# Layer two's two products by one level of Strassen's algorithm

## The chip, the cores and the metric

The kernel runs on one core of a Trainium2 chip. The metric is the device time of one execution in microseconds (us), as the median of several runs. The core's engines are TensorE (PE: matmuls, into PSUM), VectorE (DVE), ScalarE (ACT) and GpSimd (POOL); SyncE (SP) issues all DMAs here. Each engine works off its own queue in order, and waits on semaphores for the others.

## The reference

Attention over chunks of 32 tokens, with 4 x 8 heads of 768 tokens, gives 3072 rows of 512 numbers. Two feed-forward layers follow, each with 512 x 2048 and 2048 x 512 weights, all in float32:

```python
x = attn_out.transpose(0, 2, 1, 3).reshape(B * S, H * D)      # 3072 x 512
h = x @ w_in1;  g = np.maximum(0.01 * h, h);  x = g @ w_out1  # layer one
h = x @ w_in2                                                 # layer two
g = h * np.clip(h + 3.0, 0.0, 6.0) / 6.0
return (g @ w_out2).astype(np.float32)
```

## The kernel before

**Numbers.** Every operand of a feed-forward matmul is split in two parts, a high one in a rounded format that PE takes at full pace and the low remainder; a product is three matmuls (high x high, high x low, low x high), made by `mm3` (L607 to L609). A matmul has 128 x 128 weights and 512 moving columns.

**Tiling.** The 3072 tokens are 6 blocks of 512 (`blk`), the 2048 hidden features are 16 slices of 128 (`f`). A step (`layer, blk, f`) is a hidden product `hidden` (4 slices of the inner dimension x 3 = 12 matmuls into one PSUM bank `ph`), an activation on ACT and DVE (`act_1` to `act_4`, L625 to L655) that leaves the two parts `gh` and `gl`, and the output product `output` (12 matmuls into four banks `py`, which gather over the 16 steps of a block). PE runs hidden(n), then output(n - 1). `done` and `stored` copy the four banks out and store them, in layer one to `y_dram`, from where `load_y`, `split_yh` and `split_yl` fetch a block for layer two.

**Weights.** `convert` loads each 128 x 512 piece of the weights, 64 in all, which come as the bits of float64 numbers, turns them to float32 with two ACT and four DVE instructions, and splits them (`w_high`, `w_low`). The 16 slices of a layer stay in SBUF (ring `w`); layer two's are converted during the last block of layer one and the first steps after it.

**Attention.** While PE works on block b of layer one, ACT, DVE and GpSimd prepare block b + 1; PE is lent to them in short visits (`visit`).

**Order.** `Program` (L45) is a list scheduler in the kernel's own text: every step has an engine, a planned length (table `TIME`), a due time, steps that it comes after, and places in rings of buffers that it takes and frees. `order` plays this plan through and emits the instructions of each engine in the planned order; on the chip only the order is kept, and the waits are the real ones.

## Time and profile before

| | us |
|---|---|
| median of 3 runs (1135.38 to 1135.52) | 1135.45 |
| span of the profiled execution | 1133.9 |
| PE busy | 1121.4 |
| DVE busy | 589.1 |
| ACT busy | 463.7 |
| GpSimd busy | 60.4 |
| DMA moved | 78.65 MB |

The profiled execution lies 1.55 us under the median, since its span runs from the first to the last instruction only. Busy time of PE is no measure of its pace: matmuls overlap, and each is shown with its own end. The distance between equal events of a repeating pattern is.

### The profile page before, as it was taken

The numbers are of one execution on the slowest core, as the hardware profiler recorded it, in microseconds if no ns is written. First come the engines' busy times: TensorE is split into PE (matmuls) and PEld (weight loads), VectorE is DVE, ScalarE is ACT, GpSimd is POOL, SyncE is SP. The second block draws the span as 40 slices with busy tenths as digits, with TensorE's granted clock in tenths as the row PEclk, the third lists the DMA queues.
The fourth block names the chain that finished last, engine by engine and source line by source line (L and its number), as shares of the span: only waits on it lengthen the run. The fifth ranks groups of instructions, "written<-read, shape, count | busy, mean of one in ns | idle before, by whom it ended". The sixth has DMA issues, their size and how long they took to land.

```text
span 1133.9 us, 16167 instructions
## 1 busy us (share of the span) xinstructions
PE 1121.4 (99%) x6375; PEld 921.9 (81%) x6375; DVE 589.1 (52%) x1280; ACT 463.7 (41%) x1043; POOL 60.4 (5%) x123
## 2 busy tenths in 40 slices
PE   8999999999999999999999999999999999999998
PEld 6777788888888888888888888888888888888887
DVE  6999865465665556656998623223223223222222
ACT  7888732334333343335777423223223223222222
POOL 4111110001000001000000000000000000000000
PEclk9999999999999999999999999999999999999999
DMA  8656421121111122115455102002002001001001
GB/s 261 193 173 188 148 75 38 38 88 63 38 56 57 48 65 76 38 64 185 150 150 179 62 1 75 1 1 75 1 1 75 1 1 38 1 1 38 1 1 38
DMA packets 31661, 78.65 MB, mean 69 GB/s; under 512 B 3424, under 2 KB 3424, under 8 KB 31584
## 3 DMA queue, kind: packets, MB, share of 16 engines
...
## 4 chain that ended last, share of the span: by engine, by line
PE 91%; DVE 4%; ACT 2%; DMA 1%; issue 1%; POOL 1%; SPq 0%; POOLq 0%; DVEq 0%
PE py L609 44%; PE ph L609 44%; PE px L472 2%; PE psc L346 1%; ACT e L422 1%; DMA raw<-in_moe_w_in_dram 1%; DVE w L259 1%; DVE wa L240 1%; DVE raw L247 1%; DVE wa L229 0%; DVE wa L233 0%; POOL e L441 0%; DVE gl L651 0%; DMA raw<-in_moe_w_out_dram 0%; ACT w L253 0%
## 5 line engine op out<-in xcount | busy, mean ns | idle before, releaser
L609 PE MATMUL ph<-xh,w 128*128 128x512 f32 x768 | 254.6, 392 | 0.0
L609 PE MATMUL ph<-yh,w 128*128 128x512 f32 x768 | 252.0, 389 | 0.0
L609 PE MATMUL py<-gh,w 128*128 128x512 f32 x768 | 239.2, 392 | 1.0 <-DVE w L259 1.0
L609 PE MATMUL py<-w,gh 128*128 128x512 f32 x768 | 236.4, 389 | 0.0
L637 DVE SCALAR_TENSOR_TENSOR ph<-g,ph 128x512 f32<-128x512 f32 x96 | 66.8, 696 | 294.1 <-ACT g L631 294.1
L631 ACT ACTIVATE g<-ph,three 128x512 f32<-128x512 f32 x96 | 66.2, 690 | 300.0 <-PE ph L609 299.7
L609 PEld LDWEIGHTS ph<-xh,w 128*128 128x128 f32 x768 | 143.9, 188 | 30.9 <-DVE w L259 0.4
L609 PEld LDWEIGHTS py<-gh,w 128*128 128x128 f32 x768 | 142.9, 188 | 31.6 <-DVE w L259 1.7
L609 PEld LDWEIGHTS ph<-yh,w 128*128 128x128 f32 x768 | 144.2, 188 | 29.9
L609 PEld LDWEIGHTS py<-w,gh 128*128 128x128 f32 x768 | 144.2, 188 | 29.9
L609 PE MATMUL ph<-xl,w 128*128 128x512 f32 x384 | 149.6, 390 | 0.8 <-DVE xl L494 0.8
L609 PE MATMUL py<-gl,w 128*128 128x512 f32 x384 | 149.6, 390 | 0.0
L609 PE MATMUL py<-w,gl 128*128 128x512 f32 x384 | 149.4, 389 | 0.0
L609 PE MATMUL ph<-yl,w 128*128 128x512 f32 x384 | 149.4, 389 | 0.0
L628 ACT ACTIVATE ph<-ph 128x512 f32<-128x512 f32 x96 | 55.9, 582 | 179.7 <-PE ph L609 179.5
L451 DVE STREAM_TRANSPOSE aT<-e 32x128 f32<-32x128 f32 x384 | 115.9, 302 | 16.4 <-POOL e L441 11.0
L651 DVE TENSOR_TENSOR gl<-ph,gh 128x512 fp32r<-128x512 f32 x96 | 66.3, 690 | 73.2 <-ACT gh L642 72.2
L653 DVE SCALAR_TENSOR_TENSOR gl<-ph,gh 128x512 fp32r<-128x512 f32 x96 | 66.4, 691 | 55.6 <-ACT gh L644 55.6
L609 PEld LDWEIGHTS ph<-xl,w 128*128 128x128 f32 x384 | 72.1, 188 | 15.6 <-DVE xl L494 1.1
L609 PEld LDWEIGHTS py<-gl,w 128*128 128x128 f32 x384 | 72.1, 188 | 15.1
L609 PEld LDWEIGHTS py<-w,gl 128*128 128x128 f32 x384 | 72.0, 187 | 15.1
L609 PEld LDWEIGHTS ph<-yl,w 128*128 128x128 f32 x384 | 72.0, 188 | 15.0
...
## 6 DMA issues: line engine op xcount, KB each, us to landing
...
y_dram<-yo SPq DMA_DIRECT2D x24, 256.0 KB, 2.0
...
out_dram<-oo SPq DMA_DIRECT2D x24, 256.0 KB, 2.8
...
```

The costliest lines, as they stand in the source:

```text
L240: nc.vector.scalar_tensor_tensor(out=a, in0=hi, scalar=0xC0000000, in1=a, op0=ALU.bitwise_and, op1=ALU.bitwise_or)
L247: nc.vector.tensor_tensor(out=hi, in0=tmp_t.pop(key), in1=lo, op=ALU.add)
L259: nc.vector.tensor_tensor(out=w[:, io, 1, :], in0=a, in1=w[:, io, 0, :].bitcast(F32), op=ALU.subtract)
L346: nc.tensor.matmul(pt[j][n * PT:(n + 1) * PT, m * W:(m + 1) * W], qt[r, hp, :], kt[r, hp, :], start=not more, stop=True, tile_position=(e ...
L451: nc.vector.transpose(out=t[c, :, r], in_=e[r, :, c])
L472: nc.tensor.matmul(pt[e * D:(e + 1) * D, at + hp * every:at + hp * every + PT], vt[:, c], t[:, hp, n * PT:(n + 1) * PT], start=True, stop= ...
L609: nc.tensor.matmul(dst, a, b, start=first and i == 0, stop=last and i == len(terms) - 1)
L628: nc.scalar.activation(out=ph, in_=ph, func=AF.Prelu, alpha=0.01)
L631: nc.scalar.activation(out=g, in_=ph, func=AF.Relu, bias=three, scale=1.0)
L637: nc.vector.scalar_tensor_tensor(out=ph, in0=g, scalar=6.0, in1=ph, op0=ALU.min, op1=ALU.mult)
L651: nc.vector.tensor_sub(out=gl, in0=ph, in1=gh.bitcast(F32))
L653: nc.vector.scalar_tensor_tensor(out=gl, in0=ph, scalar=1.0 / 6.0, in1=gh.bitcast(F32), op0=ALU.mult, op1=ALU.subtract)
```

## The change

Layer one is computed as before. Layer two goes through its 6 blocks as 3 stages of two blocks (1024 tokens). Each of its two products is cut into 2 x 2 blocks, and 7 products of sums of these blocks take the place of 8 (in Winograd's form, with four sums of each operand).

**Weight sums.** `combine` (16 times, during blocks 1 to 4 of layer one) loads two pieces of layer two's weights, converts them, makes four sums of 128 x 256, and stores the seven operands in `w_dram`. `add_weights` fetches them two at a time as `cw0` to `cw27` when layer one's slots in `w` come free, splits them on ACT and DVE for the hidden product, and later on ACT and GpSimd for the output.

**Activation sums.** `add_x` loads 1024 tokens of `y_dram` into four tiles `rows0` to `rows3`, and makes the seven operands in place with four `mix` on DVE, each split by `high` (ACT) and `low` (DVE) of 128 x 1024 into `fb8`, `x0` to `x3`, `xwa`, `xwb`.

**Hidden products.** `add_hidden`: for a group of two pairs of feature slices (banks k = 0 and 1), products 0 to 6 go to banks B, A, E, B, E, B, D. Copies of B and E on ACT (`copied`) and sums on DVE (`summed`) give the four blocks of h; `gate` (ACT) and `gate_by` (DVE) make the activation, GpSimd a difference of two of them, and four results go to `g_dram`. Five buffers `gated` pass them on.

**Output products.** `add_outputs`: all hidden products of the three stages come first, then the outputs. The operands come from `g_dram`, with 12 `mix` a stage, and are split by ACT and DVE into three rotating tiles (`SPIN`). Weights are the stationary operand here too, so the result stands transposed: `turned_out` transposes 32 x 32 blocks on DVE, and `out_store` stores four DMAs with pieces of 64 numbers. The host lays out `w_out2` to suit.

```diff
-    rings = dict(w=NF, raw=NRAW, wa=2, ye=4, aT=2, gh=2, gl=2, x=2, py=4, ph=2, pa0=1, pa1=1, qk=1, v=1, yn=1)
+    rings = dict(w=2 * NF, raw=NRAW, wa=2, ye=4, aT=2, g=2, x=4, py=4, ph=2, pa0=1, pa1=1, qk=1, v=1)
...
+    PROD, LETTERS, FINAL = 7, "BAEBEBD", "ABEAEAD"
...
+    def h_product(p, i, c):
+        dst = sums(LETTERS[i], p % 2)
+        n = p * PROD + i
+        w, (xh, xl) = combined(n // 2)[:, n % 2], wide(c)
+        for k in range(2):
+            wh, wl = (w[:, h, k * P:(k + 1) * P] for h in range(2))
+            mm(dst, wh, xh[:, k, :], i in (0, 1, 2, 6) and k == 0)
+            mm(dst, wh, xl[:, k, :], False)
+            mm(dst, wl, xh[:, k, :], False)
+    def o_product(i, q, c):
+        w, (xh, xl) = combined(i * NQ // 2 + q // 2)[:, q % 2], wide(c)
+        for m in range(2):
+            dst = sums(FINAL[i], m)
+            wh, wl = (w[:, h, m * P:(m + 1) * P] for h in range(2))
+            mm(dst, wh, xh[:, q % 2, :], i in (0, 1, 2, 6) and q == 0)
+            mm(dst, wh, xl[:, q % 2, :], False)
+            mm(dst, wl, xh[:, q % 2, :], False)
+    def copied(n, letter, k):
+        nc.scalar.copy(out=small(n), in_=sums(letter, k))
+    def summed(letter, k, n, out):
+        b, t = sums(letter, k), small(n)
+        nc.vector.tensor_tensor(out=t if out else b, in0=b, in1=t, op=ALU.add)
...
+    def gate(letter, k, n):
+        nc.scalar.activation(out=gated(n), in_=sums(letter, k), func=AF.Relu, bias=half, scale=1.0 / 6.0)
+    def gate_by(letter, k, n):
+        g = gated(n)
+        nc.vector.scalar_tensor_tensor(out=g, in0=g, scalar=1.0, in1=sums(letter, k), op0=ALU.min, op1=ALU.mult)
+    def g_differ(a, b):
+        nc.gpsimd.tensor_tensor(out=gated(a), in0=gated(b), in1=gated(a), op=ALU.subtract)
...
+    def turned_out(k, n, m):
+        t = fixed(f"gated{k}", [P, 2, 512], "g", 2).rearrange("p a c -> p (a c)").rearrange("p (j m b) -> p j m b", j=16, m=2)
+        nc.vector.transpose(out=t[:, :, m, :], in_=small(n).rearrange("p (j b) -> p j b", b=32))
+    def out_store(k, s, n, h, i):
+        t = fixed(f"gated{k}", [P, 2, 512], "g", 2).rearrange("p a c -> p (a c)").rearrange("p (j e) -> p j e", j=16)
+        at = (2 * s + n) * TB
+        dst = out[at:at + TB, P * i + 64 * h:P * i + 64 * (h + 1)].rearrange("(j a) e -> a j e", a=32)
+        nc.sync.dma_start(out=dst, in_=t[32 * i:32 * (i + 1)])
...
+    def combine(p, io, t):
+        hold = [max((x for x in paced if x[0] <= t - 10))[1]]
+        mixed, b = [], None
+        was = [("wa", (1, 2 * p + e, io)) for e in range(2)]
+        for e in range(2):
+            key = (1, 2 * p + e, io)
+            r = ("raw", 2 + e)
+            u = t + 4 * e + LATER
+            first = [("raw", ("f", e))] if p == io == 0 else []
+            cell("SP", T["load"], u - LATER - 9, w_load, *key, after=hold, takes=first, writes=[r], nbytes=P * 4096)
+            b = cell("ACT", T["words"], u - 4.9, w_upper, key, after=[b], reads=[r], takes=was[e:e + 1])
+            l = cell("ACT", T["words"], u - 4.2, w_lower, key, writes=[r])
+            c = add("DVE", T["clip"], u - 4.2, w_clip, key, after=[b])
+            c = add("DVE", T["shift"], u - 3.7, w_shift, key, after=[c])
+            c = cell("DVE", T["join"], u - 3.2, w_join, key, after=[c], reads=[r])
+            mixed.append(cell("DVE", T["add"], u - 2.4, w_add, key, after=[c, l], reads=[r]))
+        m = ("raw", 2)
+        c = cell("DVE", T["quarter"], t + LATER + 2.5, c_first, p, io, after=mixed, writes=[m])
+        for n in range(3):
+            c = cell("DVE", T["quarter"], t + LATER + 3.0 + 0.5 * n, c_more, p, io, n, writes=[m], frees=was if n == 2 else ())
+        c_stored[io, p] = []
+        for n in range(4):
+            c_stored[io, p].append(
+                cell("SP", T["load"], t + 3.0 + 0.5 * n, c_store, p, io, n, after=mixed, reads=[m] if n > 1 else [],
+                     frees=was[n:n + 1], nbytes=P * (1024 if n == 1 - io else 2048))
+            )
...
+    WIDE = ["fb8", "x0", "x1", "xwa", "xwb", "x2", "x3"]
+    SPIN = ["xwa", "xwb", "fb8"]
+    def add_weights(io, t, need):
+        w = [("cw", t)]
+        pairs = {(2 * t + e) // PROD if io == 0 else (2 * t + e) % NQ for e in range(2)}
+        cell("SP", T["load"], need - 24, cw_load, io, t, writes=w, nbytes=P * 2048,
+             **merged(own("w", f"cw{t}"), dict(after=[x for p in pairs for x in c_stored[io, p]])))
+        cell("ACT", T["high"], need - 9, cw_high, t, writes=w)
+        if io == 0:
+            cell("DVE", T["low"], need - 8, cw_low, t, nc.vector, writes=w)
+        else:
+            cell("POOL", T["pool"], need - 8, cw_low, t, nc.gpsimd, writes=w)
+    def add_wide(src, c, need):
+        cell("ACT", T["wide_copy"], need - 4.0, high, src, c, reads=[src], writes=[c], **wide_own(c))
+        cell("DVE", T["wide"], need - 2.9, low, src, c, reads=[src], writes=[c])
...
+    def add_x(s):
+        t = hidden_at[s] - (14 if s == 0 else 3)
+        R = [("raw", j) for j in range(4)]
+        for j in (0, 2, 1, 3):
+            k, n = j // 2, j % 2
+            cell("SP", T["load"], t - 24 + j, rows_load, s, j, writes=[R[j]], nbytes=P * 4096,
+                 after=[attended] + [evicted[2 * s + n, 2 * k + e] for e in range(2)])
...
+        split(0, 0)
+        split(1, 2)
+        mixed(2, 1, 3, 1, ALU.subtract)
+        split(2, 1)
...
+    def add_hidden(s, pairs, t0):
+        keep = {}
+        for i in range(PROD):
+            for p in pairs:
+                k = p % 2
+                t = t0 + (2 * i + k) * H6
+                b, e = [(LETTERS[i], k)], t + H6
+                last = s == NS - 1 and p == NF // 2 - 1 and WIDE[i].startswith("x") and not WIDE[i].startswith("xw")
+                cell("PE", H6, t, h_product, p, i, WIDE[i], reads=[("cw", (p * PROD + i) // 2), WIDE[i]], writes=b,
+                     frees=[("x", WIDE[i])] if last else (), **bank_own(LETTERS[i], k))
+                n = {0: SA, 2: SA, 3: SB, 5: SC}.get(i)
+                if n:
+                    cell("ACT", T["copy"], e, copied, n[k], LETTERS[i], k, reads=b, writes=[n[k]], **small_own(n[k]))
+                n = {1: SA, 4: SB, 5: SA, 6: SC}.get(i)
+                if n:
+                    cell("DVE", T["sum"], e + 0.2, summed, LETTERS[i], k, n[k], False, reads=[n[k]], writes=b)
+                    g = add_gate(s, p, LETTERS[i], k, e + 1.0)
+                    if i in (1, 4):
+                        add_store(0 if i == 1 else 1, s, p, g, e + 3)
+                    elif i == 5:
+                        keep[p] = g
+                    else:
+                        cell("POOL", T["pool"], e + 2.5, g_differ, g, keep[p], reads=[("gated", keep[p])], writes=[("gated", g)])
+                        add_store(3, s, p, keep[p], e + 3)
+                        add_store(2, s, p, g, e + 4)
...
+    def add_turned(s, k, n, h, S, t, after=()):
+        for m in range(2):
+            cell("DVE", T["turn_out"], t + 0.8 * m, turned_out, k, S[m], m, reads=[S[m]],
+                 writes=[("gated", 2 * k), ("gated", 2 * k + 1)])
+        for i in range(4):
+            cell("SP", T["load"], t + 1.6, out_store, k, s, n, h, i, reads=[("gated", 2 * k), ("gated", 2 * k + 1)], nbytes=P * 1024)
...
+    def add_outputs(s):
+        t0 = output_at[s]
+        for i in range(PROD):
+            for w in range(NQ // 2):
+                need = t0 + (i * NQ + 2 * w) * H6
+                q1 = ("raw", w)
+                q2, q3 = ("x", "b", w), ("x", "t", w)
...
+                def mixed(dst, x, y, op):
+                    cell("DVE", T["wide"], need - 5.4, mix, dst, x, y, op, reads=[x, y], writes=[dst])
+                c = SPIN[spun[0] % 3]
+                spun[0] += 1
+                if i == 0:
+                    load(0, q1, need - 14)
+                elif i == 1:
+                    load(1, q2, need - 14)
+                elif i == 2:
+                    load(2, q3, need - 14)
+                elif i == 3:
+                    mixed(q3, q3, q1, ALU.add)
+                    load(3, q1, need + 2)
+                elif i == 4:
+                    mixed(q2, q2, q3, ALU.subtract)
+                elif i == 5:
+                    mixed(q3, q1, q3, ALU.subtract)
+                add_wide([q1, q2, q3, q3, q2, q3, q1][i], c, need)
+                for e in range(2):
+                    cell("PE", H6, need + e * H6, o_product, i, 2 * w + e, c, reads=[("cw", i * NQ // 2 + w), c],
+                         writes=[(FINAL[i], 0), (FINAL[i], 1)])
+            e = t0 + (i + 1) * NQ * H6
...
+    for t in range(7, 28):
+        add_weights(0, t, hidden_at[0] + t * 2 / 7 * 9.5 - 4)
+    for s in range(NS):
+        if s:
+            add_x(s)
+        for g in range(NG // 2):
+            add_hidden(s, (2 * g, 2 * g + 1), hidden_at[s] + 2 * g * PROD * H6)
+    for t in range(28):
+        add_weights(1, t, output_at[0] + t * 2 * H6 - 20)
+    for s in range(NS):
```

PE where layer two begins, before (`ph1_0_0` is the first hidden bank of layer two, `py0_5_*` the last output banks of layer one):

```order
L609 MATMUL py0_5_3_5428<-gh0_5_14_6059,w0_14_1669 128x512 x2
L609 MATMUL py0_5_3_5428<-gl0_5_14_6070,w0_14_1669 128x512
L609 MATMUL ph1_0_0_6126<-yh0_5409,w1_0_5457 128x512
L609 MATMUL ph1_0_0_6126<-yl0_5410,w1_0_5457 128x512
L609 MATMUL ph1_0_0_6126<-yh0_5409,w1_0_5457 128x512 x2
L609 MATMUL ph1_0_0_6126<-yl0_5410,w1_0_5457 128x512
L609 MATMUL ph1_0_0_6126<-yh0_5409,w1_0_5457 128x512 x2
```

and now (`sB0`, `sA0`, ... are the banks by letter and k):

```order
L635 MATMUL py0_5_3_5708<-g0_5_14_6199,w0_14_1_1796 128x512 x3
L813 MATMUL sB0_6244<-fb8_5652,cw0_5661 128x512 x6
L813 MATMUL sB1_6256<-fb8_5652,cw3_5752 128x512 x6
L813 MATMUL sA0_6266<-x0_5678,cw0_5661 128x512 x6
L635 MATMUL py0_5_0_5705<-g0_5_15_6241,w0_15_1_1845 128x512 x3
L635 MATMUL py0_5_1_5706<-g0_5_15_6241,w0_15_1_1845 128x512 x3
L635 MATMUL py0_5_2_5707<-g0_5_15_6241,w0_15_1_1845 128x512 x3
L635 MATMUL py0_5_3_5708<-g0_5_15_6241,w0_15_1_1845 128x512 x3
L813 MATMUL sA1_6298<-x0_5678,cw4_5773 128x512 x6
L813 MATMUL sE0_6313<-x1_6231,cw1_5715 128x512 x6
L813 MATMUL sE1_6327<-x1_6231,cw4_5773 128x512 x6
```

Three products of layer two now stand ahead of layer one's last output, and a row of them is six matmuls into one bank.

DVE in block 4 of layer one, before (`aT46` and `aT47` are attention transposes, `gl` the low part of an activation):

```order
L651 TENSOR_TENSOR gl0_4_12_5196<-ph0_4_12_5150,gh0_4_12_5184 128x512
L451 STREAM_TRANSPOSE aT46_5179<-e46_5112 32x4x32 x3
L451 STREAM_TRANSPOSE aT47_5186<-e47_5117 32x4x32 x3
L451 STREAM_TRANSPOSE aT46_5179<-e46_5112 32x4x32 x3
L451 STREAM_TRANSPOSE aT47_5186<-e47_5117 32x4x32 x3
L451 STREAM_TRANSPOSE aT46_5179<-e46_5112 32x4x32 x3
L651 TENSOR_TENSOR gl0_4_13_5241<-ph0_4_13_5201,gh0_4_13_5230 128x512
```

and now (`wa1_14_1` and `wa1_15_1` are pieces of layer two's weights in `combine`; `g0_4_12` is the former `gl0_4_12`):

```order
L662 TENSOR_TENSOR g0_4_12_5472<-ph0_4_12_5438,g0_4_12_5472 128x512
L255 TENSOR_SCALAR wa1_14_1_5478<-wa1_14_1_5478 128x512
L259 TENSOR_SCALAR wa1_14_1_5478<-wa1_14_1_5478 128x512
L266 SCALAR_TENSOR_TENSOR wa1_14_1_5478<-rows2_1950,wa1_14_1_5478 128x512
L276 ISA wa1_14_1_5478<-rows2_1950,wa1_14_1_5478 128x1024
L255 TENSOR_SCALAR wa1_15_1_5488<-wa1_15_1_5488 128x512
L259 TENSOR_SCALAR wa1_15_1_5488<-wa1_15_1_5488 128x512
L266 SCALAR_TENSOR_TENSOR wa1_15_1_5488<-rows3_1952,wa1_15_1_5488 128x512
L476 STREAM_TRANSPOSE aT46_5467<-e46_5399 32x4x32 x3
L662 TENSOR_TENSOR g0_4_13_5518<-ph0_4_13_5491,g0_4_13_5518 128x512
```

Seven conversion steps moved in between the two activations, and most transposes of the pair behind the second.

ACT where block 0 of layer two gives way to block 1, before:

```order
L644 ACTIVATE gh1_0_14_6711<-ph1_0_14_6683 128x512
L631 ACTIVATE g1_0_15_6734<-ph1_0_15_6715,three_67 128x512
L711 CAST yh2_6736<-yn2_6369 128x512 x2
L644 ACTIVATE gh1_0_15_6748<-ph1_0_15_6715 128x512
L711 CAST yh2_6736<-yn2_6369 128x512 x2
L631 ACTIVATE g1_1_0_6778<-ph1_1_0_6752,three_67 128x512
L684 COPY oo0_1_6787<-py1_0_1_6207 128x512
L644 ACTIVATE gh1_1_0_6791<-ph1_1_0_6752 128x512
```

and now in the third group of the first stage (`small_*` are the copies, `gated*` the gates):

```order
L835 COPY small_ye0_6355<-sB0_6244 128x512
L835 COPY small_ye1_6364<-sB1_6256 128x512
L842 ACTIVATE gated1_6373<-sE0_6313,half_73 128x512
L842 ACTIVATE gated4_6405<-sE1_6327,half_73 128x512
L835 COPY small_ye2_6390<-sB0_6244 128x512
L835 COPY small_ye3_6403<-sB1_6256 128x512
L842 ACTIVATE gated0_6324<-sB0_6244,half_73 128x512
L842 ACTIVATE gated0_6324<-sB1_6256,half_73 128x512
L842 ACTIVATE gated1_6373<-sD0_6396,half_73 128x512
L835 COPY small_wa0_6263<-sB0_6244 128x512
L842 ACTIVATE gated1_6373<-sD1_6408,half_73 128x512
L835 COPY small_wa1_6273<-sB1_6256 128x512
```

What were an activation, a split and copies of one step is now a round of copies and gates for two banks of a letter at a time.

DVE at the same change of blocks, before:

```order
L637 SCALAR_TENSOR_TENSOR ph1_0_14_6683<-g1_0_14_6702,ph1_0_14_6683 128x512
L653 SCALAR_TENSOR_TENSOR gl1_0_14_6713<-ph1_0_14_6683,gh1_0_14_6711 128x512
L637 SCALAR_TENSOR_TENSOR ph1_0_15_6715<-g1_0_15_6734,ph1_0_15_6715 128x512
L716 TENSOR_TENSOR yl2_6737<-yn2_6369,yh2_6736 128x512 x2
L653 SCALAR_TENSOR_TENSOR gl1_0_15_6759<-ph1_0_15_6715,gh1_0_15_6748 128x512
L716 TENSOR_TENSOR yl2_6737<-yn2_6369,yh2_6736 128x512 x2
L637 SCALAR_TENSOR_TENSOR ph1_1_0_6752<-g1_1_0_6778,ph1_1_0_6752 128x512
L682 COPY oo0_0_6789<-py1_0_0_6206 128x512
L653 SCALAR_TENSOR_TENSOR gl1_1_0_6802<-ph1_1_0_6752,gh1_1_0_6791 128x512
```

and now where stage 0 gives way to stage 1 (`xwal` is the low part of one of the next stage's operands, `rows2<-` a difference):

```order
L803 TENSOR_TENSOR rows2_1950<-rows2_1950,rows1_1811 128x1024
L839 TENSOR_TENSOR sE1_6327<-sE1_6327,small_ye1_6364 128x512
L846 SCALAR_TENSOR_TENSOR gated0_6324<-gated0_6324,sE0_6313 128x512
L810 TENSOR_TENSOR xwal_6254<-rows1_1811,xwah_6253 128x1024
L839 TENSOR_TENSOR sB0_6244<-sB0_6244,small_wa0_6263 128x512
L846 SCALAR_TENSOR_TENSOR gated1_6373<-gated1_6373,sE1_6327 128x512
L839 TENSOR_TENSOR sB1_6256<-sB1_6256,small_wa1_6273 128x512
L846 SCALAR_TENSOR_TENSOR gated1_6373<-gated1_6373,sB0_6244 128x512
L839 TENSOR_TENSOR sD0_6396<-sD0_6396,small_ye2_6390 128x512
L839 TENSOR_TENSOR sD1_6408<-sD1_6408,small_ye3_6403 128x512
L846 SCALAR_TENSOR_TENSOR gated4_6405<-gated4_6405,sB1_6256 128x512
L846 SCALAR_TENSOR_TENSOR gated0_6324<-gated0_6324,sD0_6396 128x512
```

Operations on 1024 columns for the next stage stand between the sums and gate products of the last group.

## Rows read from the trace of the kernel before

**Rows 1.** The page: span, busy time by engine, and granted clock in 40 slices
```profile
span 1133.9 us, 16167 instructions
PE 1121.4 (99%) x6375; PEld 921.9 (81%) x6375; DVE 589.1 (52%) x1280; ACT 463.7 (41%) x1043; POOL 60.4 (5%) x123
PEclk9999999999999999999999999999999999999999
```
**Rows 2.** The page: the chain that ended last, by engine
```profile
PE 91%; DVE 4%; ACT 2%; DMA 1%; issue 1%; POOL 1%; SPq 0%; POOLq 0%; DVEq 0%
```
**Rows 3.** Timeline (start us, us, engine, line): four blocks' output copies, layer two's start
```profile
237.47 0.68 DVE L682 COPY yo<-py 128x512 f32<-128x512 f32 x1
333.04 0.68 DVE L682 COPY yo<-py 128x512 f32<-128x512 f32 x1
605.02 0.39 PE L609 MATMUL ph<-yh,w 128*128 128x512 f32 x1
783.34 0.68 DVE L682 COPY oo<-py 128x512 f32<-128x512 f32 x1
870.38 0.68 DVE L682 COPY oo<-py 128x512 f32<-128x512 f32 x1
```
**Rows 4.** Windows: busy us (count) of PE, PEld, DVE, ACT, POOL; clock, DMA, GB/s
```profile
75.00:100.00 25.00, 24.72 (x166) 19.28 (x165) 24.32 (x51) 20.98 (x49) 3.19 (x5) 1.00 0.62 193
275.00:300.00 25.00, 25.00 (x188) 20.65 (x183) 13.96 (x41) 8.48 (x26) 2.06 (x4) 1.00 0.14 43
700.00:725.00 25.00, 25.00 (x112) 20.71 (x111) 6.94 (x10) 6.45 (x10) 0.00 (x0) 1.00 0.05 18
```
**Rows 5.** Groups by line and form: busy us, mean ns of one, idle before
```profile
L240 DVE SCALAR_TENSOR_TENSOR wa<-raw,wa 128x512 uint32<-128x512 uint32 x64 | 44.2, 690 | 1.3
L247 DVE CUSTOM_DVE_ANT_0 raw<-raw,wa 128x1024 uint16<-128x1024 uint16 x64 | 44.5, 695 | 1.5
L229 DVE TENSOR_SCALAR wa<-wa 128x512 f32<-128x512 f32 x64 | 28.3, 442 | 2.7 <-ACT wa L219 2.7
L494 DVE TENSOR_TENSOR xl<-px,xh 128x256 fp32r<-128x256 f32 x9 | 3.7, 409 | 0.0
L716 DVE TENSOR_TENSOR yl<-yn,yh 128x512 fp32r<-128x512 f32 x24 | 15.5, 684 | 0.2 <-ACT yh L711 0.2
L711 ACT CAST yh<-yn 128x512 fp32r<-128x512 f32 x24 | 13.7, 620 | 0.0
```
**Rows 6.** Timeline, late in layer two: a product, its activation, the next step
```profile
1113.43 0.39 PE L609 MATMUL ph<-yh,w 128*128 128x512 f32 x1
1113.86 0.69 ACT L631 ACTIVATE g<-ph,three 128x512 f32<-128x512 f32 x1 [3.39 <-PE ph L609]
1114.58 0.70 DVE L637 SCALAR_TENSOR_TENSOR ph<-g,ph 128x512 f32<-128x512 f32 x1 [3.39 <-ACT g L631]
```
**Rows 7.** Timeline: a GpSimd and a VectorE instruction that overlap
```profile
110.75 0.83 POOL L441 TENSOR_TENSOR e<-e,su 128x384 f32<-128x384 f32 x1 [1.68 <-DVE su L437]
110.84 1.29 DVE L259 TENSOR_TENSOR w<-raw,w 128x512 fp32r<-128x512 f32 x1 [0.23 <-ACT w L253]
```
**Rows 8.** By line: duration ns min/median/max, of two lines
```profile
L259 DVE TENSOR_TENSOR w<-raw,w x64: 675/685/1318, 22.2 to 641.9; 128x512 fp32r<-128x512 f32 x64
L651 DVE TENSOR_TENSOR gl<-ph,gh x96: 675/692/694, 38.0 to 603.9; 128x512 fp32r<-128x512 f32 x96
```
**Rows 9.** Timeline: the last stores' issue, the last matmul, the last copy
```profile
1128.87 2.27 SPq L693 DMA_DIRECT2D out_dram<-oo  x4
1129.77 0.39 PE L609 MATMUL py<-w,gl 128*128 128x512 f32 x1
1130.19 0.59 ACT L684 COPY oo<-py 128x512 f32<-128x512 f32 x1 [0.77 <-PE py L609]
```
**Rows 10.** The page's DMA issues: count, KB each, median us to landing
```profile
y_dram<-yo SPq DMA_DIRECT2D x24, 256.0 KB, 2.0
out_dram<-oo SPq DMA_DIRECT2D x24, 256.0 KB, 2.8
```

More of the change, by code (lines that the diff above doesn't have):

```diff
@@ L543, in attention @@
             before = [values_done[x] for x in [pr - 5] if x >= 0]
[L544 removed]
+            c = add("PE", T["scores"] + 0.3 * direct, due(0), a_scores, pr, after=[a] + before + set_up, takes=s, frees=qk)
         elif not two:
@@ new lines, in place, with mix, high, low @@
+    def place(c):
+        return rows(c[1]) if c[0] == "raw" else later(c[1], c[2])
+    def mix(dst, x, y, op):
+        nc.vector.tensor_tensor(out=place(dst), in0=place(x), in1=place(y), op=op)
+    def high(src, c):
+        nc.scalar.copy(out=wide(c)[0], in_=place(src))
+    def low(src, c):
+        h, l = wide(c)
+        nc.vector.tensor_tensor(out=l, in0=place(src), in1=h.bitcast(F32), op=ALU.subtract)
+    def mm(dst, a, b, start):
+        nc.tensor.matmul(dst, a, b, start=start, stop=True, skip_group_check=True)
```

383 lines of the change are left out of this document (258 added, 125 removed).

## Prediction

> **What bounds the kernel now.** The page comes first: TensorE (PE) is busy for 99% of the span at a granted clock of 1.00, that is 2.4 GHz, in every slice [rows 1], and 91% of the chain that ended last is PE work [rows 2]. Its busy time overlaps itself (each matmul is shown as 0.39 us), so the pace is read from the timeline: two equal copies of layer two lie 870.38 − 783.34 = 87.04 us apart, one block of 16 × 24 = 384 matmuls, or 226.7 ns each [rows 3]. Layer two begins at 605.02 [rows 3]; six blocks of 87.04 are 522.2 us. Nothing is left to gain there but matmuls. The windows then say what room the others have: VectorE (DVE) is busy for 6.94 of 25 us in layer two, 13.96 in the mixed blocks of layer one, 24.32 in block 0, where PE is still busy for 24.72 [rows 4]. The profiled span is 1133.9 us [rows 1]; the median of the runs is 1.55 more, and I add that at the end.
>
> **Fewer matmuls.** Layer two has 2304 matmuls now. After the change it has 3 stages × 8 pairs × 7 products × 6 = 1008 for the hidden product and as many for the output, 2016. The order shows them in the old form (128x128 weights, 512 columns, six in a row into one bank), so I keep 226.7 ns: 288 × 0.2267 = **65.3 us off the path**. That the change does not do what it says is excluded by this count.
>
> **Hidden stage, steady state.** A group of 14 products takes 14 × 1.36 = 19.04 us. Around it DVE has 8 sums and 8 gate products of about 0.69 [rows 6, 8], 11.0 us (58%), and ScalarE (ACT) 8 copies of 0.59 [rows 9] and 8 gates of 0.69 [rows 6], 10.2 us. Shares alone do not decide; one chain does. Bank B is written by product 5 and overwritten by product 0 of the next group, three products or 4.08 us later, and in between it must be copied, summed, gated and multiplied. Take 0 as 0.227 after the start of its last matmul. ACT can begin 0.20 later (1113.43 to 1113.86 [rows 6]), hand-overs between engines cost 0.03 to 0.05. The copy of bank B0 is done by 0.85; ACT then copies B1, which PE ends at 1.36, until 2.15; the gate of B0 runs to 2.88, its product on DVE to 3.61. That leaves 0.47 us, and B1, by the same walk, 0.45. **Cost taken: 0**; bounds 0 and 12 us (below).
>
> **Where two stages meet.** Eleven operations on 1024 columns (splits and differences of the next activations) enter DVE. One on 512 columns takes 684 ns, 620 on ACT [rows 5]; since 256 columns take 409 [rows 5], 512 more cost about 0.54, and I take 1.22 on DVE, 1.05 on ACT. The order puts one split (xwal) between gate product E0 and sum B0. In the walk sum B0 then ends 0.02 after the bank is due and its product at 0.71, so PE waits 0.76; ACT's copy of x3, ahead of the second gate, costs another 0.71; a difference between the two sums of the next group 0.75. That is 2.2 us a meeting, twice: 4.4. With 0.6 for GpSimd (next part), **5.0**, bounds 0 and 10.
>
> **The shared port.** In the trace a GpSimd product that runs 0.83 from 110.75 overlaps a VectorE subtraction of two SBUF tensors issued at 110.84, and this takes 1.29 instead of 0.685 [rows 7, 8]: it waited 0.6. The subtractions of a PSUM and an SBUF tensor (L651) never exceed 0.694 [rows 8]. The Trainium skill, page "SBUF — State Buffer", section "Who interferes with whom", says that a VectorE instruction with two SBUF inputs and a GpSimd instruction that reads SBUF lock each other out for a whole instruction. The trace agrees; by page and row alike 28 GpSimd splits beside wide operations would cost DVE 17 us, so the place decides. The change adds 28 splits and 24 differences to GpSimd, and 33 + 120 wide operations with two SBUF inputs to DVE. The order lets nearly all 28 splits run in the last hidden stage, where DVE's sums and gate products take one operand from PSUM; only the first five meet wide operations. So 0.6 us in the sum and a rival.
>
> **Output stage.** Its 56 products take 76.2 us. DVE has 28 splits and 12 differences of 1.22 (48.8), 8 sums and 8 transposes of 0.69 (11.0): 59.8 us, 79%. The tight part is products 2 to 5: 28 × 1.22 + 8 × 0.69 = 39.7 in 43.5. Three buffers let a split run up to two pairs of products (5.4 us) ahead. Walked in the order's sequence, with the first split 2.9 us early, the tightest split (product 3, third pair) is ready 0.5 us before PE needs it. **Cost 0**; the bound from doubling 684 ns to 1.37 is 28 × 0.15 = 4.2 a stage, less a margin of 0.5: 11 us.
>
> **Weight sums in layer one.** Each of 16 combinations costs DVE 2 × (0.44 + 0.44 + 0.69 + 0.695) + 4 × 0.41 = 6.2 us [rows 5]. The layer-two conversions that they replace stood later, in block 5, so nothing is taken off here. Four fall on a block of 95.57 us (237.47 to 333.04 [rows 3]): 26% on top of 56% [rows 4], 82%, and with the port lock (8 GpSimd products a block, 0.6 each) 87%. PE's order in layer one is unchanged but for the last attention visit (`px48`), 18 matmuls later. Block 0 shows PE losing 0.28 of 25 us at 97% DVE [rows 4]; over the 380 us of four blocks that would be 4 us. I take **1.5**, bounds 0 and 8 (if the longer DVE queue stalls visits twice as much). No gain is possible, as PE has no idle time there. The stores and reloads of the weights have tens of us of lead and land in 2 to 3 us [rows 10]; they cost nothing unless a queue head blocks.
>
> **The end.** The last matmul starts at 1129.77, so its nominal end is 1130.00, and the span ends 3.9 later; the last copy ends at 1130.78, and 3.1 of that are its store [rows 1, 9]. Now sum, two transposes and the wait take 2.3 us, then four stores at once: before, four took 2.27 us to issue, copies included [rows 9], so 0 to 1.7 more; I take 1.0. Pieces of 256 bytes instead of 2 KB have no row; landing of 2.0 to 2.8 [rows 10] at most doubled gives 0 to 2.8, I take 1. That is 7.4 against 3.9: **3.5**, bounds 1.5 and 6.
>
> **Sum.** 1133.9 − 65.3 + 5.0 + 1.5 + 3.5 = 1078.6; with 1.55, **1080** us, 4.9% less.
>
> **Rivals.** *The bank chain is late in every group.* Against it: the walk leaves 0.47 us. For it: the hand-overs of rows 6 come from an ACT that had waited 3.39 us, not from a loaded one. At 1 us a group, 12 groups: 1092. *Layer one pays*, at twice the loss of block 0: 1088. *The port lock hits in the output stage*: if the 28 splits slipped there, 0.8 each (0.6 on 384 columns, scaled to 512), that is 22 us more on DVE, 59.8 + 22 = 82 against 76, and more in the tight part: up to 10 us, 1090. The page named above gives this rule; the order speaks against the place. *Slower*: VectorE bounds the output stage. This needs wide operations above (76.2 − 11) / 40 = 1.63 us; from 2.09 us on, 3 × (40 × 2.09 + 11 − 76.2) = 55 eats the gain. At 2.2, 1148. Only a lock on every one of them would do that.
>
> **How the numbers follow.** Forecast 1080 (1073 to 1087) 74%, bank chain 10%, layer one 6%, lock 4%, slower 3%, others 3%. The lower end has all small terms at 0 and the end at 1.5 (1071.7); the upper end takes in the first three rivals: 1071 to 1094. A measurement of this kernel tells 0.2% from no change; the forecast and three rivals are faster by far more: 95%, within 1%, slower 4%.
>
> **What would show it.** PE: 42 matmuls per 9.52 us in layer two; PE waits on "ACT gated" or "DVE gated" only where stages meet, about 2 us each; in the output stage no wait on the splits; the first layer-two product near 606; from the last matmul to the end 7 us. Wrong if matmuls are spaced wider than 227 ns without a named wait, or if waits recur every 19 us.

## The result: 1076.1 us, and the profile after

| | before | after |
|---|---|---|
| median, us | 1135.41 (4 runs, 1135.15 to 1135.52) | 1076.12 (4 runs, 1074.67 to 1076.48) |
| span of the profiled execution, us | 1133.9 | 1074.2 |

The ratio is 0.9472, with a 95% interval of 0.9459 to 0.9486: 59.3 us less, where 55 were forecast (1080).

The page of the changed kernel, where [rows 1, 2] answer (span; busy time by engine; granted clock; chain that ended last):

```profile
span 1074.2 us, 16739 instructions
...
PE 1057.4 (98%) x6087; PEld 868.2 (81%) x6087; DVE 794.5 (74%) x1505; ACT 568.7 (53%) x1160; POOL 131.2 (12%) x175
...
PEclk9999999999999999999999999999999999999999
...
PE 87%; DVE 5%; ACT 3%; DMA 2%; issue 1%; POOL 1%; SPq 0%; DVEq 0%; POOLq 0%; ACTq 0%
```

PE still sets the pace, although VectorE went from 52 to 74%. Windows in layer one, a hidden stage, the first meeting of two stages, and the output (columns as in [rows 4]):

```profile
275.00:300.00 25.00, 25.00 (x208) 20.64 (x202) 21.10 (x56) 10.48 (x29) 2.06 (x4) 1.00 0.40 131
650.00:675.00 25.00, 25.00 (x112) 20.71 (x111) 15.32 (x23) 14.68 (x24) 3.88 (x3) 1.00 0.31 116
675.00:700.00 25.00, 25.00 (x112) 20.68 (x111) 22.23 (x27) 16.50 (x25) 3.52 (x2) 1.00 0.53 171
875.00:900.00 25.00, 25.00 (x112) 20.71 (x111) 19.61 (x19) 10.57 (x11) 0.00 (x0) 1.00 0.57 152
```

PE is never idle in them. The timeline gives the two ends of layer two (start us, us, engine, line, operation):

```profile
605.94 2.88 PE L813 MATMUL sB<-fb,cw 128*128 128x512 f32 x12
...
1063.74 2.88 PE L813 MATMUL sD<-fb,cw 128*128 128x512 f32 x12
```

Between the two groups of PE lie 457.80 us. 2004 matmuls of layer two and the last 12 of layer one start in that time: 2016 x 0.2267 = 457.0, so all of layer two lost 0.8. Behind block 0 of layer one PE has two waits (engine, line, waited for: us in total, times, longest):

```profile
PE ph L635 <- DVE g L662: 0.6, 1, 0.6
PE sB L813 <- DVE gated L846: 0.6, 1, 0.6
```

The account of the profiled execution: 65.3 us of matmuls gone; layer one 0.9 longer (605.94 against 605.02 [rows 3]; 0.85 of it lies between the output copies of blocks 1 and 2, see below); 0.8 for the second of these waits; and from the nominal end of the last matmul (1063.74 + 12 x 0.2267 = 1066.46) to the end 7.7 instead of 3.9, 3.8 more. That is −59.8; the spans differ by 59.7. The forecast had 5.0 us for the two meetings of stages. PE has no wait at either: that is the gap to explain.

### The profile page after: what moved, and what is told of

It is laid out like the page before. It is cut to its first block, busy times and chain, and to the rows that moved or that the text cites. A ratio compares the mean times of both kernels' runs of the same rounds, so it can differ in the third digit from the quotient of the medians.

```text
span 1074.2 us, 16739 instructions
## 1 busy us (share of the span) xinstructions
PE 1057.4 (98%) x6087; PEld 868.2 (81%) x6087; DVE 794.5 (74%) x1505; ACT 568.7 (53%) x1160; POOL 131.2 (12%) x175
## 4 chain that ended last, share of the span: by engine, by line
PE 87%; DVE 5%; ACT 3%; DMA 2%; issue 1%; POOL 1%; SPq 0%; DVEq 0%; POOLq 0%; ACTq 0%
PE py L635 21%; PE ph L635 21%; PE sA L813 12%; PE sE L813 12%; PE sB L813 12%; PE sD L813 6%; PE px L497 2%; PE psc L371 1%; ACT e L447 1%; DMA raw<-in_moe_w_in_dram 1%; DVE raw L278 1%; DVE w L287 1%; DVE wa L266 1%; DVE aT L476 1%; DMA cw<-w_dram 1%
## 5 line engine op out<-in xcount | busy, mean ns | idle before, releaser
L635 PE MATMUL py<-g,w 128*128 128x512 f32 x1152 | 280.2, 391 | 0.9 <-DVE w L287 0.8
L635 PEld LDWEIGHTS py<-g,w 128*128 128x128 f32 x1152 | 214.8, 188 | 46.7 <-DVE w L287 1.7
L476 DVE STREAM_TRANSPOSE aT<-e 32x128 f32<-32x128 f32 x384 | 116.0, 302 | 16.4 <-POOL e L466 10.9
L662 DVE TENSOR_TENSOR g<-ph,g 128x512 fp32r<-128x512 f32 x96 | 66.1, 689 | 43.0 <-ACT g L657 41.8
L657 ACT CAST g<-ph 128x512 fp32r<-128x512 f32 x96 | 56.4, 587 | 18.4 <-PE py L635 15.6
L447 ACT ACTIVATE e<-e,mx 128x96 f32<-128x96 f32 x140 | 50.6, 364 | 8.4 <-DVE mx L407 8.4
L813 PE MATMUL sE<-xwbh,cw 128*128 128x512 f32 x160 | 52.5, 389 | 0.0
L813 PE MATMUL sB<-fb,cw 128*128 128x512 f32 x192 | 46.6, 390 | 0.6 <-DVE gated L846 0.6
L466 POOL TENSOR_TENSOR e<-e,su 128x384 f32<-128x384 f32 x48 | 42.0, 887 | 11.5 <-DVE su L462 9.1
L813 PE MATMUL sB<-xwah,cw 128*128 128x512 f32 x128 | 42.0, 389 | 0.0
L792 POOL TENSOR_TENSOR cw<-cw 128x512 fp32r<-128x512 f32 x28 | 37.4, 1346 | 33.8 <-ACT cw L788 26.0
```

The costliest lines, as they stand in the source:

```text
L447: nc.scalar.activation(out=e[:, hp, :], in_=p_t[pr][j][:, m * W:(m + 1) * W] if direct else e[:, hp, :], func=AF.Exp, scale=SCALE if direc ...
L466: nc.gpsimd.tensor_tensor(out=e, in0=e, in1=su.unsqueeze(2).to_broadcast([P, HP, W]), op=ALU.mult)
L476: nc.vector.transpose(out=t[c, :, r], in_=e[r, :, c])
L635: nc.tensor.matmul(dst, a, b, start=first and i == 0, stop=last and i == len(terms) - 1)
L657: nc.scalar.copy(out=g[:, 0, :], in_=ph_t[key])
L662: nc.vector.tensor_sub(out=g[:, 1, :], in0=ph, in1=g[:, 0, :].bitcast(F32))
```

## Experiments

Each is one edit of the changed kernel, whose layer two takes 457.0 us, measured as above, where nothing stalls. The kernels with one edit were executed once each. The first product of layer two moves between 605.5 and 606.7 from one execution to the next where layer one is the same, so effects are read inside a trace and not from the difference of two times.

### The order at the meetings

```diff
-                cell("PE", H6, t, h_product, p, i, WIDE[i], reads=[("cw", (p * PROD + i) // 2), WIDE[i]], writes=b,
-                     frees=[("x", WIDE[i])] if last else (), **bank_own(LETTERS[i], k))
+                chain["mm"] = cell("PE", H6, t, h_product, p, i, WIDE[i], reads=[("cw", (p * PROD + i) // 2), WIDE[i]], writes=b,
+                                   frees=[("x", WIDE[i])] if last else (), **merged(bank_own(LETTERS[i], k), dict(after=[chain.get("mm")])))
```

> PE's products of the hidden stages are kept in the written order. In the changed kernel as it is, PE takes A0, B0, A1, B1 at the first products where two stages meet; here it takes B0, B1, A0, A1 there as everywhere else (one more such swap falls in the second group of the second stage). Nothing else is changed. Theory 1 (the order hid the meetings): in the trace of the changed kernel the gate product of bank B0 ends at 684.83 and that of B1 at 687.35, while PE would now want B0 at 684.82 and B1 at 686.18. So each of the two meetings costs waits of 0.1 and 1.2 us plus restarts, 1.5 to 2.2 us; the span grows from 1074.2 to 1077.2 to 1078.6. The walk of the prediction gave 2.2 per meeting, the same size. Theory 2 (the walk was too slow, because VectorE passes a 512-column operation every 0.60 us and not every 0.69, and the swap does not matter): no wait on bank B at the meetings and a span of 1074.2 within 0.3.

Span 1077.3; layer two takes 460.42, 3.4 us more than 457.0. At the first meeting in the changed kernel, PE, VectorE and ScalarE:

```profile
682.10 2.88 PE L813 MATMUL sD<-x,cw 128*128 128x512 f32 x12
684.82 1.52 PE L813 MATMUL sA<-x,cw 128*128 128x512 f32 x6
686.18 1.52 PE L813 MATMUL sB<-fb,cw 128*128 128x512 f32 x6
687.54 1.52 PE L813 MATMUL sA<-x,cw 128*128 128x512 f32 x6
688.90 1.52 PE L813 MATMUL sB<-fb,cw 128*128 128x512 f32 x6
...
681.22 1.22 DVE L810 TENSOR_TENSOR xwal<-rows,xwah 128x1024 fp32r<-128x1024 f32 x1
682.36 0.69 DVE L839 TENSOR_TENSOR sB<-sB,small_wa 128x512 f32<-128x512 f32 x1
...
684.15 0.68 DVE L846 SCALAR_TENSOR_TENSOR gated<-gated,sB 128x512 f32<-128x512 f32 x1
...
686.68 0.69 DVE L846 SCALAR_TENSOR_TENSOR gated<-gated,sB 128x512 f32<-128x512 f32 x1 [0.65 <-ACT gated L842]
...
685.01 1.06 ACT L806 CAST x<-rows 128x1024 fp32r<-128x1024 f32 x1 [1.24 <-PE sD L813]
685.98 0.68 ACT L842 ACTIVATE gated<-sB,half 128x512 f32<-128x512 f32 x1
```

The cast for x3 (685.01) does stand ahead of the second gate, and bank B1 is free only at 687.37, as the walk of the prediction had it. But PE takes A0 first, then B0, A1, B1, and wants B1 at 688.90. In the written order it wants B1 1.36 behind B0, at 686.81 on that run's clock:

```profile
682.66 2.88 PE L813 MATMUL sD<-x,cw 128*128 128x512 f32 x12
685.45 1.65 PE L813 MATMUL sB<-fb,cw 128*128 128x512 f32 x6
687.99 1.66 PE L813 MATMUL sB<-fb,cw 128*128 128x512 f32 x6 [0.89 <-DVE gated L846]
689.49 2.88 PE L813 MATMUL sA<-x,cw 128*128 128x512 f32 x12
```

A is due at 682.66 + 24 x 0.2267 = 688.10 and starts at 689.49, 1.39 late; at the second meeting it is 1.38. A third wait, listed with 0.31 at 783.90, makes up the rest of the 3.4; it stands a group later and is taken up under the late weight load. Theory 1 holds: the planner's swap hid the meetings, 2.8 us in all.

### The room of the bank chain

```diff
-        nc.scalar.activation(out=gated(n), in_=sums(letter, k), func=AF.Relu, bias=half, scale=1.0 / 6.0)
+        for _ in range(times):
+            nc.scalar.activation(out=gated(n), in_=sums(letter, k), func=AF.Relu, bias=half, scale=1.0 / 6.0)
...
-                    g = add_gate(s, p, LETTERS[i], k, e + 1.0)
+                    g = add_gate(s, p, LETTERS[i], k, e + 1.0, 3 if i == 5 else 1)
```

> In the hidden stages the gate activation of the two B banks of product 5 is done three times instead of once on ScalarE (same values, same place in its queue), 1.16 us more in the chain that frees bank B. Theory 1 (the walk of the prediction, 0.47 us left): a wait of 0.7 us in each of 12 groups. Theory 2 (the trace of the changed kernel: B0's gate product ends at 646.12, its next matmul starts at 646.74, 0.57 left after a hand-over): a wait of 0.6 us in each group, and since a wait shown as 0.6 made PE 0.84 late in the two places where one stands in the changed kernel, 0.85 per group, 10 us in all, a span of about 1084. If a wait costs just what the view shows, 7 us: 1081. If the chain had much more room than the walk said, nothing: 1074.2.

Span 1091.2, layer two 474.17: 17.2 us more, and all numbers expected were too small. One group, ScalarE, VectorE and PE:

```profile
647.14 4.16 ACT L843 ACTIVATE gated<-sB,half 128x512 f32<-128x512 f32 x6
...
649.31 0.69 DVE L847 SCALAR_TENSOR_TENSOR gated<-gated,sB 128x512 f32<-128x512 f32 x1 [1.33 <-ACT gated L843]
...
646.46 2.88 PE L813 MATMUL sD<-x,cw 128*128 128x512 f32 x12
650.05 1.67 PE L813 MATMUL sB<-fb,cw 128*128 128x512 f32 x6 [0.71 <-DVE gated L847]
652.07 1.66 PE L813 MATMUL sB<-fb,cw 128*128 128x512 f32 x6 [0.35 <-DVE gated L847]
653.57 1.75 PE L813 MATMUL sA<-x,cw 128*128 128x512 f32 x7
```

The same place in the changed kernel, ScalarE's gate and VectorE's gate product of bank B0:

```profile
644.70 0.69 ACT L842 ACTIVATE gated<-sB,half 128x512 f32<-128x512 f32 x1
...
645.44 0.68 DVE L846 SCALAR_TENSOR_TENSOR gated<-gated,sB 128x512 f32<-128x512 f32 x1
```

From the start of the first gate to that of the product there are 649.31 − 647.14 = 2.17 us, before the edit 0.74. So the two gates more cost 1.43, not 1.16. Bank B0 was due at 646.46 + 12 x 0.2267 = 649.18 and came at 650.05, 0.87 late: 1.43 − 0.87 = 0.56 us of room, where the walk had 0.47. The size was missed for another reason too: the second bank waits again, and PE is 653.57 − 651.90 = 1.67 late for waits of 1.06, some 0.3 more for each.

### The shared port, in the wrong place

```diff
-            cell("POOL", T["pool"], need - 8, cw_low, t, nc.gpsimd, writes=w)
+            hold = [max(multiplied.values())] if t >= 8 else []
+            cell("POOL", T["pool"], need - 8, cw_low, t, nc.gpsimd, writes=w, after=hold)
```

> 20 of the 28 splits on GpSimd (all but the first 8) are held back until the last hidden product, so that they run in the first output stage, beside VectorE's operations with two SBUF inputs. Theory 1 (the port lock hits in the output stage, the rival of the prediction): each of the 20 makes a VectorE operation 0.8 to 1.1 us longer, 16 to 22 us on top of some 56 in 76; most of it falls in the first half of the stage, and PE waits 3 to 10 us in all: a span of 1077 to 1084. The Trainium skill, page SBUF - State Buffer, section Who interferes with whom, gives this lock for every such pair. Theory 2 (GpSimd does the waiting): splits of 2.1 to 2.3 us on GpSimd, VectorE operations stay at 1.22, PE waits less than 1 us: 1074 to 1075.

Span 1082.3, layer two 465.20: 8.2 us more, as theory 1 has it. VectorE, GpSimd and PE in the first output stage:

```profile
872.77 2.31 DVE L810 TENSOR_TENSOR xwal<-ot,xwah 128x1024 fp32r<-128x1024 f32 x1
...
884.00 1.22 DVE L810 TENSOR_TENSOR xwal<-ot,xwah 128x1024 fp32r<-128x1024 f32 x1
...
845.60 32.85 POOL L792 TENSOR_TENSOR cw<-cw 128x512 fp32r<-128x512 f32 x16
...
862.55 0.39 PE L813 MATMUL sE<-xwah,cw 128*128 128x512 f32 x1
864.93 0.50 PE L813 MATMUL sE<-xwal,cw 128*128 128x512 f32 x1 [1.99 <-DVE xwal L810]
...
869.15 0.40 PE L813 MATMUL sE<-xwbh,cw 128*128 128x512 f32 x1
```

A split of the same kind takes 2.31 beside GpSimd and 1.22 once GpSimd is done (845.60 + 32.85 = 878.45); a GpSimd split takes 32.85 / 16 = 2.05 instead of 1.29. So both wait. The Trainium skill (page "SBUF — State Buffer", section "Who interferes with whom") states that such a pair contends; the trace agrees, and shows that both sides pay. PE is listed with 4.9 us of waits here (1.99, 1.5 and 1.4) and is 8.2 late. The first wait shows why: 12 matmuls, 2.72 us, lie between 862.55 and 869.15, so a wait of 1.99 made PE 6.60 − 2.72 = 3.88 late. The window after it (columns as in [rows 4]):

```profile
865.00:870.00 5.00, 5.00 (x15) 3.96 (x16) 5.00 (x6) 0.65 (x1) 5.00 (x4) 0.66 0.31 51
```

The granted clock is 0.66 there, part of it at the lower level of 1.2 GHz. Behind the two shorter waits of this run it is 1.00, as it is behind the waits of 0.55 to 0.89 us in the changed kernel and in the written order.

### The point where VectorE bounds the output

```diff
...
-                add_wide([q1, q2, q3, q3, q2, q3, q1][i], c, need)
+                add_wide([q1, q2, q3, q3, q2, q3, q1][i], c, need, 2)
```

> Every one of the 28 VectorE splits of an output stage is done twice (same result), nothing else is changed. This puts VectorE over PE's 76.2 us per stage, so that its real pace can be read off. Theory 1 (pace as the prediction charged it, 1.22 and 0.69 us an operation): 68 x 1.22 + 16 x 0.69 = 94.0 us a stage, 17.8 over, 53 us for three stages less a lead of up to 5: a span of 1122 to 1127. Theory 2 (operations in a full queue follow each other every 1.14 and 0.60 us, as read between their starts in the changed kernel): 68 x 1.14 + 16 x 0.60 = 87.1, 10.9 over, 33 less the lead: 1102 to 1107. If VectorE's waits on loads and copies add to it, more than theory 2 gives.

Span 1123.9, layer two 507.76: 50.8 us more, 16.9 a stage. VectorE is busy in nearly all of these two windows (columns as in [rows 4]):

```profile
834.00:910.00 76.00, 65.14 (x270) 50.46 (x269) 74.66 (x71) 31.53 (x39) 11.57 (x7) 0.98 0.48 148
910.00:1002.00 92.00, 79.87 (x337) 62.12 (x336) 89.68 (x85) 33.60 (x37) 0.00 (x0) 1.00 0.44 115
```

Two of its pairs of splits in the timeline:

```profile
903.82 2.48 DVE L811 TENSOR_TENSOR fb<-ot,fb 128x1024 fp32r<-128x1024 f32 x2
906.21 2.48 DVE L811 TENSOR_TENSOR xwal<-ot,xwah 128x1024 fp32r<-128x1024 f32 x2
```

The span lies in theory 1's range, but not for its reason. A pair takes 2.39 from start to start. An operation on another tile follows a split after 1.14 (681.22 to 682.36 above), so the second split of a pair, which writes the tile of the first again, starts 1.25 after it. That the common tile is the reason isn't shown. So which pace holds without repeats can't be told by this run. It does tell the bound: the prediction's sum with the doubled splits gives 94.0 − 76.2 = 17.8 a stage, and 16.9 were paid. The doubling put 28 x 1.25 = 35.0 us on VectorE in a stage, so some 18 of them found room, where the prediction's sum leaves 76.2 − 59.8 = 16.4.

### The wait in layer one

```diff
...
-        nc.vector.tensor_tensor(out=t[:, o, :], in0=x, in1=y, op=op)
+        nc.vector.tensor_tensor(out=t[:, o, :32], in0=x[:, :32], in1=y[:, :32], op=op)
```

> The 64 additions and subtractions that make the weight sums in layer one work on 32 columns instead of 256; the order of all queues stays. (The weight sums are thereby left out for the most part, and layer two computes something else.) It takes some 20 us from VectorE in blocks 1 to 4. In the changed kernel layer two begins at 605.94 instead of 605.02, and one wait of 0.56 us at 243.75 stands for it, in which a subtraction for g was behind 15 transposes of the attention. Theory 1 (the load that the sums put on VectorE makes this wait): it goes, and layer two begins at 605.0 to 605.2; the span falls to 1073.3. Theory 2 (the place of the transposes in VectorE's queue makes it, which the planner chose when it fitted the sums in): the wait stays within 0.2 of its size, and layer two begins at 605.8 to 606.

Layer two begins at 606.13, and the wait is there:

```profile
243.90 0.50 PE L635 MATMUL ph<-xh,w 128*128 128x512 f32 x1 [0.55 <-DVE g L662]
```

So the load of the sums is not its cause. (The conversions, the larger part of what `combine` puts on VectorE, stayed.) The timelines of VectorE in block 2, before the change and after it, show another difference:

```profile
238.18 3.77 DVE L451 STREAM_TRANSPOSE aT<-e 32x128 f32<-32x128 f32 x12
241.98 0.69 DVE L651 TENSOR_TENSOR gl<-ph,gh 128x512 fp32r<-128x512 f32 x1
```

```profile
238.24 4.73 DVE L476 STREAM_TRANSPOSE aT<-e 32x128 f32<-32x128 f32 x15
243.00 0.69 DVE L662 TENSOR_TENSOR g<-ph,g 128x512 fp32r<-128x512 f32 x1
```

The plan with the weight sums puts 15 instead of 12 transposes ahead of the subtraction that frees PE's bank. So they were put back:

```diff
+    for step in program.steps:
+        if step[3] is a_turn and step[4] in ((24, 3), (25, 3)):
+            step[5].append(acts[0, 2, 1][1])
```

> In block 2 of layer one the last two groups of three transposes of pairs 24 and 25 are put behind the subtraction for g; one w_clip of 0.43 us comes ahead of it instead, and nothing else moves on VectorE, PE or GpSimd. In the kernel before, 12 transposes stand ahead of this subtraction, which starts at 241.98; in the changed kernel 15, and it starts at 243.00, with the wait of 0.56 us. Theory 1 (the third group of transposes that the new plan put ahead is the whole cost of the weight sums in layer one): the subtraction starts 0.5 earlier, the wait is 0 to 0.1, and the output copies of block 1 and 2 lie 95.6 to 95.7 us apart, as before the change (95.57), instead of 96.42. Theory 2 (VectorE is just fuller, and another instruction is late next): 96.0 to 96.4.

```profile
238.74 3.76 DVE L476 STREAM_TRANSPOSE aT<-e 32x128 f32<-32x128 f32 x12
242.53 0.43 DVE L255 TENSOR_SCALAR wa<-wa 128x512 f32<-128x512 f32 x1
242.87 0.68 DVE L662 TENSOR_TENSOR g<-ph,g 128x512 fp32r<-128x512 f32 x1
```

The listed wait is gone, and the copies of blocks 1 and 2 lie 95.80 apart (238.02, 333.82), against 96.42 after (237.53, 333.95) and 95.57 before [rows 3]. That is between the ranges of the two theories and near the first: of the 0.85 us that layer one lost, 0.62 were the place of three transposes. 0.23 remain, most likely because the clip now stands there.

### The late weight load

In the last hidden stage of the changed kernel ScalarE's timeline reads:

```profile
776.69 0.62 ACT L788 CAST cw<-cw 128x512 fp32r<-128x512 f32 x1 [1.74 <-DMA cw<-w_dram]
777.22 0.68 ACT L842 ACTIVATE gated<-sE,half 128x512 f32<-128x512 f32 x1
```

A cast waits at the head of the queue for a load that took 5.98 us to land (2.9 in the median), the gate behind it is late, and PE waits for bank B at 780.73.

```diff
...
+            hold = [made[min(made.index(last) + 7, len(made) - 1)]]
-        cell("ACT", T["high"], need - 9, cw_high, t, writes=w)
+        cell("ACT", T["high"], need - 9, cw_high, t, writes=w, after=hold)
```

> In the last hidden stage ScalarE's cast of each reloaded weight is put at least 7 products (9.5 us) behind the last product that reads the old one; nothing is left out. In the changed kernel one such cast waited at the head of ScalarE's queue until 776.69 for a load issued at 770.69, the gate of bank E1 behind it came 1.7 us late, and PE waited 0.55 us for bank B at 780.73, 0.84 late in all. Theory 1 (the load, 5.98 us to landing instead of 2.9 beside two loads of 512 KB, is the cause): the wait goes and the span falls by 0.8 to 1073.4. Theory 2 (it is the end of the meeting, VectorE catching up after the wide operations): the wait stays, 1074.2.

Layer two takes 456.95, without a wait. But the runs with other ends and the repeat of the changed kernel have none there either (456.96 and 457.03 in two of them), with the casts where they were. All traces together show more. In seven of them with the same casts and the same order in this stage, the same cast waits 0.33 to 1.23 us for its load, and PE doesn't wait. Where it waited 1.74, PE waited 0.55; in the written order a cast waited 2.13 (it starts at 778.19), and the third wait of PE there, 0.31, follows. In the three kernels with the casts moved no cast of this stretch waits for a load. So PE waits only where that load came late by more than 1.23, which points to the load; that the edit wins time in the median isn't shown.

### The end

```diff
+            end = i % 2 and s == NS - 1 and n == h + 1 == k == 1
-            cell("SP", T["load"], t + 1.6, out_store, k, s, n, h, i, reads=[("gated", 2 * k), ("gated", 2 * k + 1)], nbytes=P * 1024)
+            cell("ACT" if end else "SP", T["load"], t + 1.6, out_store, k, s, n, h, i, nc.scalar if end else nc.sync, reads=[("gated", 2 * k), ("gated", 2 * k + 1)], nbytes=P * 1024)
```

> Of the last four stores two are issued by ScalarE instead of SyncE, nothing else is changed. In the changed kernel the last transpose ends at 1068.56, the last of the four issues starts at 1070.0 and the span ends at 1074.2. Theory 1 (four issues in a row on one queue cost what the prediction charged, 0 to 1.7 us, here 1.4): the last store is issued about 0.9 earlier, and from the last matmul to the end there are 6.8 us instead of 7.7. Theory 2 (the landing alone counts, pieces of 256 bytes on the same DMA engines): no change, 7.7.

The last matmul group starts at 1062.93 and the span is 1073.4: 7.7 from its end, as before. ScalarE's two issues start at 1067.78, behind the last transpose (1066.45 + 1.29), and all four issues are over at 1068.71, 3.06 behind the last matmul's end; in the changed kernel they take until 1070.81, 4.35 behind it. Nothing is won by that, as theory 2 has it. What holds the end instead, behind the issue, isn't shown.

```diff
...
+                if s == NS - 1 and i == PROD - 1 and w == NQ // 2 - 1:
+                    for m in range(2):
+                        for e in range(2):
+                            cell("PE", H6 / 2, need + m * H6, o_product, i, 2 * w + e, c, (m,), reads=[("cw", i * NQ // 2 + w), c],
+                                 writes=[(FINAL[i], m)])
+                    continue
```

> Of the last 12 matmuls the 6 for bank D0 come first, then the 6 for bank D1; before, the two banks took turns. Nothing is left out. In the changed kernel VectorE's two last sums start at 1065.98, when D0 is whole, and with two transposes end at 1068.56. Theory 1 (VectorE's four operations in a row set the end): the sum and transpose of D0 run while PE still works on D1, and 2 x 0.6 us go out of the way, less the wait for D1's end: from the last matmul to the end 7.1 us instead of 7.7. Theory 2 (the sums are held by the last matmul of both banks anyway): no change.

VectorE:

```profile
1064.03 0.69 DVE L839 TENSOR_TENSOR small_ye<-sD,small_ye 128x512 f32<-128x512 f32 x1 [4.04 <-PE sD L813]
1064.75 0.71 DVE L859 STREAM_TRANSPOSE gated<-small_ye 128x512 f32<-128x512 f32 x1
1065.39 0.69 DVE L839 TENSOR_TENSOR small_ye<-sD,small_ye 128x512 f32<-128x512 f32 x1
1066.11 0.71 DVE L859 STREAM_TRANSPOSE gated<-small_ye 128x512 f32<-128x512 f32 x1
```

The first sum now starts at 1064.03, while PE still works. The last group starts at 1062.47, its end is 1065.19, the span 1072.4: 7.2, half a microsecond won, as theory 1 has it. The two kernels below that hold this edit have 7.2 as well.

### The edits together

> The changed kernel once more, as the reference for the run beside it: 1075 to 1077, and a second look at two waits. The wait of 0.56 us for g in block 2 of layer one was there in all seven profiles so far and should be there again; that for bank B behind a late weight load stood in the changed kernel's profile alone of those that keep its casts and its orders (not in the runs with other ends), so it is expected to be absent or somewhere else.

> The changed kernel with the last 12 matmuls bank by bank and the casts of reloaded weights put 7 products behind, both together. From the run with the end alone: 0.5 us less behind the last matmul. From the casts: 0 to 0.8, as the wait that they avoid comes in some executions only. In all 0.5 to 1.3 us less than the changed kernel, 1074.8 to 1075.6 if that takes 1076.1; if the end is held by the landing of the stores after all, no difference.

> The changed kernel with the three edits together: the transposes behind the subtraction, the last 12 matmuls bank by bank, the casts of reloaded weights later. From their single runs 0.8, 0.5 and 0 to 0.8 us less: 1074.0 to 1074.9, against 1076.1 to 1076.2 for the changed kernel and 1075.4 with the last two alone. If the wait in layer one only moves elsewhere: 1075.4.

| | median, us | runs | ratio to before, 95% |
|---|---|---|---|
| changed kernel, again | 1076.20 | 4 (1075.99 to 1077.31) | 0.9474 (0.9461 to 0.9487) |
| end and casts | 1075.39 | 5 (1074.95 to 1075.84) | 0.9465 (0.9452 to 0.9478) |
| end, casts and transposes | 1074.34 | 5 (1073.54 to 1076.17) | 0.9463 (0.9450 to 0.9475) |

The repeat has the wait in layer one (0.55) and none for bank B. The medians fall by about what the traces show, but the intervals overlap: that the last version is faster than the changed kernel is likely from the traces and not proved by the times.

## Why the forecast held, and where its steps did not

- **Matmuls.** Right: layer two passes 2016 matmuls in 457.03 us without a stall, 226.7 ns each.
- **Steady hidden groups.** Right: no wait but the one of the late load, and room of 0.56 us (0.47 by the walk).
- **Meetings, 5.0 us.** Wrong, and nearly all of the 4 us between forecast and result. The walk timed the banks at a meeting, but let PE take them in the steady groups' order; the order of PE's queue has A0 ahead of B0 there, which gives bank B 1.36 us more and B1 twice that. In the written order a meeting costs 1.4, not 2.2. The walk was also slow: it charged 0.69 an operation in a full VectorE queue, where sums and gate products start every 0.60 (682.36 to 684.15 holds three). So in the written order B0 comes 0.07 late (685.45, due at 682.66 + 2.72), where the walk had 0.76; and the 0.75 for the next group came in neither order. The GpSimd lock was there, 2.31 instead of 1.22 on one operation of each meeting, where nobody waited.
- **Port lock.** The place was right. The price was 1.1 rather than 0.8 an operation. The rival, where up to 10 us were forecast for 28 splits, cost 8.2 with 20 of them moved; some 1.7 of these were lost behind the first wait at the lower clock, which the prediction had not counted.
- **Output stage.** Right: no wait in three stages. The tightest split ends 0.9 us ahead of its products (907.81, 908.70), where the walk had 0.5.
- **Layer one, 1.5 us.** 0.85 came. The reason given, a fuller VectorE, was wrong for most of it: 0.62 were three transposes put ahead of one subtraction by a new plan. (The rival's 1088 adds its 8 us to a forecast that already holds 1.5; its own terms give 1086.7.)
- **The end, 3.5 us.** 3.8 came. That issues of stores cost up to 1.7 is not borne out: two on each of two queues won nothing.
- **A blocked queue head.** The prediction named it as the condition under which reloads of weights cost something, and put it at nothing. It came: a cast ahead of a gate in ScalarE's queue, waiting for a load, cost 0.8 us in the profiled execution, and in the repeat nothing.
- **Median above span.** 1.55 was added; it was 1.9. Of the eight executions of the changed kernel seven took 1.8 to 2.1 us longer than their span, and one, the profiled one of the repeat, 3.4; why isn't known.

The misses other than the meetings, −0.65, +0.3, +0.8 and +0.4, add up to under 1 us because they have different signs; that much of the agreement is luck. Of the signs that the prediction named, one failed: no wait of about 2 us where stages meet. The others came: 226.7 ns a matmul, no wait on the splits, the first product at 605.94, 7.7 us at the end.
